# Filling TensorE's two gaps in the head: ten dummy matmuls in one group, two short ones ahead of the first transposes, six between the first and the second

## The chip, the cores and the metric

The kernel runs on one core of one Trainium2 chip. The metric is the device time of one execution in microseconds (us), as the median of several runs. A profiled execution is a separate run; it gives the page, the timeline and the waits.

## The reference

One block of a transformer over x of 2048 rows and 640 columns in bf16. The rows are layer-normalised; the sum of three terms is returned: x, a sliding-window attention with 32 heads of 20 columns and a window of 256, and a gated linear unit with 1536 hidden columns.

```python
x = A_x
xn = _layernorm(x, axis=-1)
return x + _A_ref(xn, A_wqkv, A_wo) + _B_ref(xn, B_w_gate, B_w_up, B_w_down)
# _A_ref: qkv = xn @ wqkv, masked softmax(q k^T / sqrt(20)) v per head, @ wo
# _B_ref: (sigmoid(xn @ w_gate) * (xn @ w_up)) @ w_down
```

## The kernel before

The 2048 rows are worked on in four chunks of 512 (`CW`), each of four blocks of 128 rows. A chunk needs its normalised rows transposed (`xnT`), with the columns of x on the partitions; then TensorE projects v (row block by row block), q and k (`proj_block`, tile `pqk`), takes scores (`scores`, tile `ps`), multiplies the exponentials with v (`pv`, tile `acc`), and computes the gated unit (`g_gu`, tiles `pg` and `pu`) and the output (tile `y`). The order on each engine is the order in which the program issues: a manual schedule. In the main part a list of filling work (`Fill`) is pulled between the steps of scores by costs that are fixed in the program, not by times on the chip.

The change lies in the head, which is the work on chunk 0 ahead of q and k and is written out by hand. SyncE's queue first loads the four row blocks of x (0, 1 and 3, then 2, each into a slice of `xc`), the weights of v in two halves, those of q and k, and the first halves of `wg` and `wu`. Meanwhile TensorE multiplies a constant tile of ones with itself, ten times with 512 columns (line 196, tile `pwarm`), with no use of the result. Row blocks 0 and 3 get mean and variance from VectorE (lines 205 and 211); row blocks 1 and 2 get theirs from ScalarE's accumulating activations (lines 637 and 642). The root comes from ScalarE (621, 643), the reciprocal and the normalisation from VectorE (631 and 224 for blocks 0 and 3, 647 and 648 for blocks 1 and 2). TensorE then transposes a block by five matmuls of 128 columns (line 230, tile `pt`), and ScalarE or VectorE copies the result into `xnT` (line 231). The projection of v (line 301, tiles `pv` and `pvh`) takes five matmuls of 320 columns for each block and half of the columns. The order on TensorE is: dummies, transposes of block 0, of block 1, five pv of block 0, five of block 1, transposes of block 3, five pv of block 0, five of block 3, five of block 1, transposes of block 2, five pv of block 3, ten of block 2, and then the fifty pqk of q and k.

In PSUM, `ps_d` has four buffers for everything with the tag "d", among them `pwarm`, `pv`, `pqk`, `pg`, `pu`, `acc` and `y`, which are taken in turn. In the head `ps_h` has four more for `pt` and `pvh`; later these banks belong to `ps`.

Behind the head SyncE loads chunk 1 of x (line 115), which needs the buffer of chunk 0 and so waits until block 2 has been normalised (line 648). GpSimd waits for that load (`landed`, line 700) and then clears parts of the scratch of q and k in HBM (line 153). The stores of q and k (line 271), the loads that spread them over partitions (`qT`, `kT`, line 284) and the second half of the first part of `w_up` (line 156) follow in SyncE's queue.

## Time and profile before

| | |
|---|---|
| runs | 309.94, 310.18, 310.60 us; median 310.18 |
| profiled execution | 310.91 us, of which 309.2 us from its first to its last instruction |
| busy TensorE | 305.0 us of 309.2 |
| busy VectorE, ScalarE, GpSimd | 186.3, 192.8 and 83.8 us |
| matmuls | 4431, as many weight loads |
| granted TensorE clock | 1.000 for the core |
| HBM | 25.59 MB read, 11.44 MB written |

Times in the views are in microseconds from the span's start. "PE" is TensorE's matmul side and "PEld" its weight loads, "DVE" VectorE, "ACT" ScalarE, "POOL" GpSimd, "SP" SyncE. Matmuls overlap one another in the array and their ends are modelled, so the length of a group holds, besides its work, the way of the last result through the array; the distance from one start to the next is the rate. An arrow names what ended a wait. A wait of TensorE is listed only where the engine was idle by these modelled ends.

### The profile page before, as it was taken

The numbers are of one execution on the slowest core, as the hardware profiler recorded it, in microseconds if no ns is written. First come the engines' busy times: TensorE is split into PE (matmuls) and PEld (weight loads), VectorE is DVE, ScalarE is ACT, GpSimd is POOL, SyncE is SP. The second block draws the span as 40 slices with busy tenths as digits, with TensorE's granted clock in tenths as the row PEclk, the third lists the DMA queues.
The fourth block names the chain that finished last, engine by engine and source line by source line (L and its number), as shares of the span: only waits on it lengthen the run. The fifth ranks groups of instructions, "written<-read, shape, count | busy, mean of one in ns | idle before, by whom it ended". The sixth has DMA issues, their size and how long they took to land.

```text
span 309.2 us, 10136 instructions
## 1 busy us (share of the span) xinstructions
PE 305.0 (99%) x4431; PEld 169.0 (55%) x4431; DVE 186.3 (60%) x373; ACT 192.8 (62%) x184; POOL 83.8 (27%) x183
## 2 busy tenths in 40 slices
PE   8999999999999999999999999999999999999996
PEld 3654445564556655644456655654446665444774
DVE  4577548678992679577564557355383626465523
ACT  6823686888764657777674656877676466768000
POOL 5011124554314133332223132331313232231100
PEclk9999999999999999999999999999999999999999
DMA  7996939879937322540252112560000210000301
GB/s 213 344 265 192 346 90 274 226 239 310 211 125 176 119 73 87 174 137 11 78 127 63 47 58 88 167 203 2 2 2 3 66 45 23 2 2 2 87 22 64
DMA packets 35756, 36.86 MB, mean 119 GB/s; under 512 B 2944, under 2 KB 35456, under 8 KB 35712
## 3 DMA queue, kind: packets, MB, share of 16 engines
q1 hardware_dynamic: 34304, 33.84, 37.1%
q0 software_dynamic: 544, 1.61, 1.7%
q10 hardware_dynamic: 864, 0.77, 0.9%
q8 instruction: 34, 0.56, 0.8%
q14 instruction: 10, 0.08, 0.1%
HBM read 25.59 MB, written 11.44 MB: 120 GB/s over the span
## 4 chain that ended last, share of the span: by engine, by line
PE 97%; DMA 1%; ACT 1%; DVE 0%; SPq 0%; issue 0%
PE pg L411 18%; PE y L434 17%; PE pu L420 17%; PE pqk L263 14%; PE ps L497 9%; PE y L441 7%; PE acc L530 6%; PE pv L321 6%; PE pv L301 2%; DMA xc<-in_A_x_dram 1%; PE pt L230 0%; PE pvh L301 0%; ACT turn L637 0%; ACT turn L642 0%; DVE turn L648 0%; SPq L132 0%
## 5 line engine op out<-in xcount | busy, mean ns | idle before, releaser
L503 ACT ACTIVATE pT<-ps 128x2048 bf16<-128x2048 f32 x76 | 141.1, 1856 | 61.8 <-PE ps L497 56.2
L486 POOL TENSOR_SCALAR_AFFINE_SELECT pT<-pT 64x256 bf16<-64x256 bf16 (+1 forms) x120 | 67.7, 564 | 183.4 <-ACT pT L503 132.7
L411 PE MATMUL pg<-xnT,wg 128*128 128x512 bf16 x240 | 59.9, 380 | 0.0
L420 PE MATMUL pu<-xnT,wu 128*128 128x512 bf16 x240 | 59.8, 380 | 0.0
L424 DVE SCALAR_TENSOR_TENSOR h<-th,pu 128x512 bf16<-128x512 f32 x48 | 32.8, 683 | 44.4 <-ACT th L414 25.9
L434 PE MATMUL y<-wd,h 128*128 128x320 bf16 (+2 forms) x396 | 57.0, 296 | 0.0
L263 PE MATMUL pqk<-xnT,wqkv 128*128 128x512 bf16 x200 | 45.9, 381 | 0.0
L434 PEld LDWEIGHTS <-h 128*128 128x128 bf16 x396 | 36.7, 98 | 16.3 <-issue 2.5
L514 DVE TENSOR_TENSOR pT<-pT,keep 128x512 bf16<-128x512 bf16 (+1 forms) x76 | 35.3, 465 | 13.9 <-ACT pT L503 13.0
L414 ACT ACTIVATE th<-pg 128x512 f32<-128x512 f32 x48 | 28.6, 595 | 14.8 <-PE pg L411 14.3
L420 PEld LDWEIGHTS <-wu 128*128 128x128 bf16 x240 | 22.3, 98 | 27.6 <-issue 2.0
L411 PEld LDWEIGHTS <-wg 128*128 128x128 bf16 x240 | 21.7, 98 | 27.0 <-issue 3.6
L263 PEld LDWEIGHTS <-wqkv 128*128 128x128 bf16 x200 | 22.5, 119 | 19.2 <-issue 1.8
L497 PE MATMUL ps<-qT,kT 20*64 20x320 bf16 (+4 forms) x1440 | 32.2, 261 | 0.0
L445 DVE SCALAR_TENSOR_TENSOR rows<-y,rows 128x320 bf16<-128x320 f32 x30 | 14.6, 489 | 24.9 <-PE y L441 24.8
L541 DVE STREAM_TRANSPOSE t<-acc 128x512 f32<-128x512 f32 x32 | 20.9, 692 | 12.1 <-PE acc L530 12.1
L497 PEld LDWEIGHTS <-kT 20*64 20x64 bf16 x1440 | 13.1, 103 | 23.0 <-issue 21.9
L441 PE MATMUL y<-wo,oc 128*128 128x320 bf16 (+2 forms) x165 | 24.2, 295 | 0.0
L530 PEld LDWEIGHTS <-v 64*32 64x32 bf16 x1440 | 17.0, 92 | 6.7 <-issue 1.8
L530 PE MATMUL acc<-pT,v 64*32 64x320 bf16 (+4 forms) x1440 | 20.0, 253 | 0.0
L441 PEld LDWEIGHTS <-oc 128*128 128x128 bf16 x165 | 15.5, 98 | 6.5 <-issue 1.0
L321 PE MATMUL pv<-wqkv,xnT 128*64 128x320 bf16 x240 | 17.4, 300 | 0.0
(61 smaller groups left out, 177.4 us busy)
## 6 DMA issues: line engine op xcount, KB each, us to landing
qT<-sq SPq DMA_DIRECT2D x16, 256.0 KB, 4.6
kT<-sk SPq DMA_DIRECT2D x16, 256.0 KB, 5.0
xc<-in_A_x_dram SPq DMA_DIRECT2D x16, 160.0 KB, 4.0
sq<-st SPq DMA_DIRECT2D x20, 128.0 KB, 3.5
sk<-st SPq DMA_DIRECT2D x20, 128.0 KB, 2.6
out_dram<-rows SPq DMA_DIRECT2D x15, 160.0 KB, 1.8
wg<-in_B_w_gate_dram SPq DMA_DIRECT2D x4, 480.0 KB, 7.3
wu<-in_B_w_up_dram SPq DMA_DIRECT2D x4, 480.0 KB, 8.2
```

The lines of the kernel that those rows point to most:

```text
L263: nc.tensor.matmul(ps, lhsT=wt[:, m, :], rhs=xnT[c][:, :, d, :], start=(d == 0), stop=(d == DC - 1))
L321: nc.tensor.matmul(ps[hf * U:(hf + 1) * U, 0:HALF], lhsT=xnT[c][:, s, d, rows], rhs=wqkv[:, d, 2 * D + hf * HALF:2 * D + (hf + 1) * HALF], ...
L411: nc.tensor.matmul(pg, lhsT=part(wg, d, f), rhs=xnT[c][:, :, d, :], start=(d == 0), stop=(d == DC - 1))
L420: nc.tensor.matmul(pu, lhsT=part(wu, d, f), rhs=xnT[c][:, :, d, :], start=(d == 0), stop=(d == DC - 1))
L424: nc.vector.scalar_tensor_tensor(out=h, in0=th, scalar=1.0, in1=pu, op0=ADD, op1=MULT)
L434: nc.tensor.matmul(y[:, 0:cut[1] - cut[0]], lhsT=ht[c, f][:, s * P:(s + 1) * P], rhs=wd[:, f, cut[0]:cut[1]], start=(f == 0), stop=False)
L441: nc.tensor.matmul(y[:, 0:cut[1] - cut[0]], lhsT=oc[c, m][:, s * P:(s + 1) * P], rhs=wo[:, m, cut[0]:cut[1]], start=False, stop=(m == DC - 1))
L486: nc.gpsimd.affine_select(out=part, in_=part, pattern=pattern, compare_op=GE, fill=0.0, base=-1 if sign > 0 else 0, channel_multiplier=sign)
L497: nc.tensor.matmul(ps[side * U:(side + 1) * U, i, col * U:(col + n) * U], lhsT=qk["k", kc, half][32 * i:32 * i + DH, 2 * r + side, kb * U: ...
L503: nc.scalar.activation(out=pt[:, :, 0:used, :], in_=ps[:, :, 0:used * U], func=EXP, scale=SCALE)
L514: nc.vector.tensor_tensor(out=part, in0=part, in1=limit.to_broadcast([P, HG, n * U]), op=MIN)
L530: nc.tensor.matmul(accs[side][32 * i:32 * i + 32, q * U:(q + n) * U], lhsT=vt[sb][rows, b, at:at + 32], rhs=pt[rows, i, col:col + n, :], s ...
```

## The change

The loop that issued the dummies in two groups of six and four becomes a function of the number and the columns. It is called with ten of 512 columns and two of 128 columns in the old place, that is ahead of the transposes of block 0, and with six of 128 columns between the transposes of block 0 and those of block 1. Each call takes a buffer with the tag "d" from `ps_d`, so three are taken instead of two. Nothing else is edited, and the number and the order of instructions on VectorE, ScalarE, GpSimd and SyncE are those of before; TensorE has eight matmuls and eight weight loads more. Behind the inserted lines the line numbers are higher by 4, and behind the call of six by 5.

```diff
-    for n in (6, 4):
+    def warm(n, cols):
         ps = ps_d.tile([P, CW], FP32, name="pwarm", tag="d")
         for k in range(n):
-            nc.tensor.matmul(ps, lhsT=ones[:, 0:P], rhs=ones, start=(k == 0), stop=(k == n - 1))
+            nc.tensor.matmul(ps[:, 0:cols], lhsT=ones[:, 0:P], rhs=ones[:, 0:cols],
+                             start=(k == 0), stop=(k == n - 1))
+
+    warm(10, CW)
+    warm(2, P)
...
     for lo, hi in ((0, 3), (3, DC)):
         transpose_rows(0, act, lo, hi)
+    warm(6, P)
     norm_act(1, xn1, neg1, r1)
```

## The prediction

> **What bounds the kernel now.** I read the page first, for the chain that ended last and the clock row, then TensorE's waits, then the timeline of TensorE over the first 14 us, and last the chain in order of time over the first 20 us. From the page, the second line of the chain (shares of the span by engine):

> ```profile
> PE 97%; DMA 1%; ACT 1%; DVE 0%; SPq 0%; issue 0%
> ```

> TensorE's waits over the whole span (who waited, for whom, us in total, times, longest):

> ```profile
> PE pwarm L196 <- PEq L826: 0.8, 1, 0.8
> PE pt L230 <- DVE turn L648: 0.4, 1, 0.4
> ```

> The end is set by TensorE's own instructions, and after 6.5 us it has no wait that the list shows. A microsecond taken off TensorE's start is then worth a microsecond at the end, as long as its operands come that much sooner too. The timeline of TensorE (start, length, engine, line, operation, output and inputs, count, and in brackets the idle time before):

> ```profile
> 0.85 4.42 PE L196 MATMUL pwarm<-const-bfloat16-1.0 128*128 128x512 bf16 x10 [0.85 <-PEq L826]
> 5.36 0.71 PE L230 MATMUL pt<-ident,turn 128*128 128x128 bf16 x5
> 6.50 0.71 PE L230 MATMUL pt<-ident,turn 128*128 128x128 bf16 x5 [0.43 <-DVE turn L648]
> 7.01 2.87 PE L301 MATMUL pv<-wqkv,xnT 128*128 128x320 bf16 x10
> ```

> Two gaps are to be seen: 0.09 us between the dummies' end (0.85 + 4.42 = 5.27) and the first transposes, and 0.43 us (6.07 to 6.50) before the second. The chain in order of time (start, length, what):

> ```profile
> 6.00 0.46 DVE turn L648
> 6.46 0.05 issue
> 6.50 0.71 PE pt L230 x5
> 7.22 2.67 PE pv L301 x10
> 9.88 0.46 PE pt L230 x5
> 10.35 1.44 PE pv L301 x10
> 11.79 0.68 PE pvh L301 x5
> 12.46 0.28 PE pt L230 x5
> 12.74 0.68 PE pvh L301 x5
> 13.42 1.44 PE pv L301 x10
> 14.86 5.18 PE pqk L263 x24
> ```

> Here is what the change can reach. The same matmul of 320 columns takes 2.67 / 10 = 0.267 us ahead of 9.88 and 0.68 / 5 = 0.136 us behind 11.79; five transposes fall from 0.71 to 0.28. The dummies of 512 columns go at 0.43 us (their weight loads start at 1.23, 1.66 and 2.08), the projections of the same width at 5.18 / 24 = 0.216. TensorE runs at half rate until about 10.1 us, inside the third set of transposes, although the page's granted clock reads 1.00 for the core; so this step is read from durations.

> **Why the step comes at 10.1.** The unbroken stretch of 4.42 us from 0.85 did not bring it, the one of 3.6 us from 6.50 did. Length alone cannot explain that; periods on a fixed grid can, if the rate rises at the end of a period that was (nearly) all work. One such period p ends at 10.1 and began no earlier than 6.50, so p is at most 3.6; that none fits between 0.85 and 5.27 rules out 2.42 to 3.08 (10.1 - 2p at most 5.27 and 10.1 - 3p at least 0.85). I take 3.08 to 3.6. The period before it then ends between 6.5 and 7.0 and began between 2.9 and 3.9: it held both gaps, some 0.5 us idle. This is worked out from one run, so it is an estimate.

> **The change part by part.** Ten dummies in one group instead of six and four: the same instructions, back to back already, worth nothing.

> Two of 128 columns, 0.43 x 128 / 512 = 0.107 us each, 0.21 together: the ten stop issuing at about 0.85 + 10 x 0.427 = 5.1, so the two issue until 5.3; the first transposes wait for VectorE's normalised row block 0 until 5.36. Hidden by that wait; without it they cost at most 0.21.

> Six of 128 columns, 0.64 us, queued behind the first transposes. Those stop issuing at about 5.9 (5.36 + 5 x 0.107), so the six end at 6.5, and the second transposes were waiting for L648 until 6.50. Cost 0 to 0.1 as the rows stand, at most 0.64 if row block 1 were ready at once. The second dummy group takes the bank of the old one, the third takes one more of the four "d" banks: every later tile moves one place round the ring and still follows the tile four before it. The order of instructions on VectorE, ScalarE, GpSimd and SyncE is unchanged, so nothing is queued behind a new wait.

> With both gaps filled TensorE works from 0.85 on, the period ending at 6.5 to 7.0 is full, and the rate doubles there instead of at 10.1. I follow the head with the step at 6.7. The second transposes' last result comes at 7.04 (7.22 before). VectorE's copy of it (0.49) starts behind L211 at 7.10 and ends at 7.59. The first five pv (0.136 each) are out by then, the next five run 7.65 to 8.33. Block 3 is normalised at 8.15 (7.85 + 0.45 = 8.30 before, 0.15 sooner with the copy); its transposes take 8.33 to 8.61, five pv 8.61 to 9.29. VectorE's copies (0.48 of v, 0.49 of the transposes, 0.48 of v) end at 8.65, 9.29 and 9.80, then it normalises block 2 by 10.42; ScalarE's root for it is there at 9.41 as before. Ten pv run 9.35 to 10.71, the last transposes to 10.99, copied by 11.68; the last fifteen pv run 10.99 to 13.10, with a wait of 0.07 for that copy. The first pqk started at 14.70 (14.86 in the chain is the end of the one before): it starts 1.6 us sooner. Half rate itself cost more, 10 x 0.131 for pv and some 0.6 for transposes, 1.9 in all; the rest goes to VectorE's and ScalarE's steps, which keep their lengths. My bounds for this term are 1.2 (step at 7.7, copies in the way) and 1.75.

> **What must come sooner too.** SyncE's loads of the head do not move. The q weights are issued at 3.71 and land 6.8 us later, at 10.5 (needed at 13.1); the k weights 8.5 later at 12.8 (needed at 18.5); block 1's x is waited for by GpSimd's L700 until 19.6, and behind it the two clears of scratch go out at 20.13 and 20.91. The k tile of the first scores is issued at 28.43, behind the last store of k, and lands 3.4 later at 31.8; the scores stand at 33.14. That is 1.3 us of cover, and the store, being released by TensorE's own results, moves with them. The narrowest is the second half of w_up: issued at 28.86, 4.4 to landing, 33.27, against its first use at 33.49. It follows the k tile in SyncE's queue and so moves too; if the stores move 0.3 less than TensorE, I lose up to 0.1 there. Taken as 0, bounds 0 and 0.3.

> Sum: -1.6 us. The profiled execution took 310.91 us (span 309.2); it would take 309.3. The three runs' median is 310.18, 0.73 lower; on that scale 308.6, with 308.4 to 309.3 from the bounds.

> **The rivals.**
> (a) The filling does not count. The full period 6.7 to 10.1 was 2.67 us of pv and the rest transposes; the filled one would be 2.6 us of dummies and 0.7 of transposes. If dummies on constant ones, or transposes, do not count as work, the step stays near 10.1 and the time at 310.2. Against it: the two periods are alike within 0.1 us in either count. [...]
> (b) The profiled execution is not like the others: the grid lies otherwise against the start, and the timed runs of the kernel before already have the early step. Then nothing is left to gain, 310.2. For it: all three are below the profiled one. Against it: the runs lie within 0.66 us, less than half of what the step is worth, and none is 1.6 below. [...]
> (c) The gain is taken back at the first scores: the stores of q and k, 1.6 us sooner, meet a DMA that the stage table shows full (share 1.08 to 1.12 until 20 us). If the k tile moved not at all, 33.14 - 1.6 = 31.54 against 31.8 would cost 0.3, and w_up at 33.27 against 31.9 would cost 1.4: 310.0 at the worst.
> (d) Slower: the step stays at 10.1 and the dummies stand in front of transposes that are ready. It decides where x lands sooner than in this profile, so that block 1 is normalised before 6.4. Price up to 0.64 for the six and 0.21 for the two: 310.9 where most of it counts. Against it: L648 ended at 6.46 here, behind a chain through ScalarE.

> **How the numbers follow.** About 0.2% (0.62 us) is what a measurement of this kernel can tell from no change, so faster means below 309.56, slower above 310.80. Forecast 0.74; (a) 0.09, (b) 0.06 and (c) 0.04, which all end within 0.2%; (d) 0.07. The first is faster, 0.74; the next three 0.19; the last slower, 0.07. The range goes from 307.9 (the upper bound 1.75, and the runs' own spread) to 310.3, so that it takes in the rivals that gain nothing and leaves out (d).

> **What would show it.** In the changed kernel's timeline: dummies and transposes without a gap before 6.5; the ten pv behind the second transposes in some 1.5 us instead of 2.87; the first pqk near 13.1; the first scores near 31.5; no wait of TensorE at L420 or L497 ahead of 35 us. It is wrong if pv still takes 0.267 us up to 10 us (a or d), if the early step is there and the time unchanged (b), or if a wait for kT or wu appears (c).

## The result, and the profile after

The changed kernel is slower, by about 0.35%: 310.55 us median (309.73 to 312.72, 21 runs) against 309.28 us (309.19 to 310.9, 21 runs, the three of before among them), ratio 1.0035 with a 95% interval of 1.0022 to 1.0048. The kernel before, in its further runs, is mostly faster than its first three: 12 of the 21 lie between 309.19 and 309.31. The changed kernel never reaches that, and spreads over 3 us.

Its profiled execution is one of its quick ones, 309.82 us with a span of 308.0. The chain by engine, from its page:

```profile
PE 97%; DMA 1%; ACT 1%; DVE 0%; issue 0%; SPq 0%
```

The timeline of TensorE (start, length, what, count, idle before):

```profile
0.85 4.22 PE L196 MATMUL pwarm<-const-bfloat16-1.0 128*128 128x512 bf16 x12 [0.85 <-PEq L831]
5.29 0.45 PE L234 MATMUL pt<-ident,turn 128*128 128x128 bf16 x5 [0.22 <-DVE turn L228]
5.58 0.51 PE L196 MATMUL pwarm<-const-bfloat16-1.0 128*128 128x128 bf16 x6
6.43 0.45 PE L234 MATMUL pt<-ident,turn 128*128 128x128 bf16 x5 [0.34 <-DVE turn L652]
6.72 1.60 PE L305 MATMUL pv<-wqkv,xnT 128*128 128x320 bf16 x10
```

Twelve dummies now take 4.22 us where ten took 4.42, and the first transposes are already at full rate (0.45 for five, against 0.71 before): the step came during the ten wide dummies, at some 4.5 (their starts lie 0.43 us apart up to 4.22, then 0.36, and the next start follows 0.22 later), ahead of everything that was added. The six then fill only half of their gap. The chain in order of time says what the head gained:

```profile
6.43 0.45 PE pt L234 x5
6.88 1.44 PE pv L305 x10
...
13.11 10.79 PE pqk L267 x50
```

By this view, which counts from the end of the matmul before, the pqk start 1.75 us sooner (13.11 against 14.86). But the last matmul comes only 1.24 us sooner. TensorE's waits show where 0.5 us went, in the line with "issue", which the kernel before did not have:

```profile
PE pwarm L196 <- PEq L831: 0.8, 1, 0.8
PE pu L424 <- issue: 0.3, 1, 0.3
PE pt L234 <- DVE turn L652: 0.3, 1, 0.3
PE pt L234 <- DVE turn L228: 0.2, 1, 0.2
```

and in the chain for 128 to 136 us (start, length, what):

```profile
133.01 0.36 PE ps L501 x24
133.37 0.32 PE pu L424
133.69 0.35 issue
134.04 1.04 PE pu L424 x4
```

Between the first and the second of five matmuls of one accumulation TensorE stands still, with no semaphore to wait for ("issue"). From start to start it is 0.74 us instead of 0.22, so 0.52 is lost. One thing that such a wait does not name is the supply of the instructions themselves. Section 3 of the page has a DMA queue for them (queue and kind: packets, MB, share):

```profile
q8 instruction: 34, 0.56, 0.8%
```

In the trace each has 16384 bytes, and they follow TensorE's progress: from packet 0, when 217 instructions had been executed, to packet 33, at 8646, one starts for every 255.4 on average, matmuls, weight loads and a few of its sequencer together (packet 13 at 3535, packet 14 at 3790; packets are counted from 0). That a packet holds 256 instructions is my estimate from this. The stall comes after 3776 of the instructions in the trace.

### The profile page after: what moved, and what is told of

Same layout as the page of the kernel before. It is cut to its first block, busy times and chain, and to the rows that moved or that the text cites. A ratio compares the mean times of both kernels' runs of the same rounds, so it can differ in the third digit from the quotient of the medians.

```text
span 308.0 us, 10152 instructions
## 1 busy us (share of the span) xinstructions
PE 303.3 (98%) x4439; PEld 168.3 (55%) x4439; DVE 186.1 (60%) x373; ACT 192.4 (62%) x184; POOL 83.8 (27%) x183
## 4 chain that ended last, share of the span: by engine, by line
PE 97%; DMA 1%; ACT 1%; DVE 0%; issue 0%; SPq 0%
PE pg L415 18%; PE y L438 18%; PE pu L424 17%; PE pqk L267 15%; PE ps L501 9%; PE y L445 7%; PE acc L534 6%; PE pv L325 6%; PE pv L305 1%; DMA xc<-in_A_x_dram 1%; PE pvh L305 0%; PE pt L234 0%; ACT turn L641 0%; ACT turn L646 0%; DVE turn L652 0%
## 5 line engine op out<-in xcount | busy, mean ns | idle before, releaser
L501 PEld LDWEIGHTS <-kT 20*64 20x64 bf16 x1440 | 13.1, 103 | 23.2 <-issue 21.6
```

Source lines behind the costliest of these rows:

```text
L501: nc.tensor.matmul(ps[side * U:(side + 1) * U, i, col * U:(col + n) * U], lhsT=qk["k", kc, half][32 * i:32 * i + DH, 2 * r + side, kb * U: ...
```

## The experiments

**Theory F**: the 16 added instructions (eight matmuls, eight weight loads) move the borders of TensorE's code packets against a burst of short matmuls, so that a packet comes late. **Rivals**: E, the earlier head collides with DMA later; G, the short dummies themselves; and (b) of the prediction on what the head is worth. Each ratio below is against runs of the kernel before made beside the experiment; their medians lie between 309.44 and 309.64, where beside the changed kernel it was 309.28, so medians of different sets are comparable to some 0.3 us only.

**Sixteen instructions elsewhere.** The kernel before, its head untouched, with the first scores issued twice:

```diff
-            for side in range(2):
+            again = 1 if (c, pr, k, q) == (0, 0, 0, 0) else 0
+            for side in [0, 1] * (1 + again):
```

> The kernel before, with the eight matmuls of the first scores issued twice (0.12 us by 24 in 0.36); its head is that of before, but behind 31 us TensorE's instruction stream stands 16 instructions further on, as in the changed kernel. Theory F (code fetch: TensorE's stream is loaded in packets of 16 KB, and 16 more instructions move the packets' borders into a burst of short matmuls, where the next packet comes late): as spread as the changed kernel, median some 310.2 to 310.8, against 309.2 to 309.4 of before; in the profile a stall of TensorE of 0.3 to 1 us without a releaser near 135 us. Rival E (the earlier head itself collides with DMA later): like before plus 0.12, 309.3 to 309.5, no stall.

310.76 us (309.99 to 312.73, 12 runs), ratio 1.0028 (1.0009 to 1.0047). Its wait list has the stall at the same instruction, 3776, although no dummy was added and the head is that of before, which neither E nor G allows:

```profile
PE pu L420 <- issue: 0.7, 1, 0.7
```

**The changed head without the shift.** The changed kernel less eight matmuls with v:

```diff
         for n_, (pt, k, q, n, col) in enumerate(flat):
+            if (c, pr, n_) == (0, 0, 4):
+                continue
```

> The changed kernel without eight of the matmuls with v of chunk 0's first pair of heads (0.11 us by 92 in 1.26; that key block's part of the sum is left out): the head is the changed one, but behind 48 us the instruction stream is aligned as before. Theory F: tight again, 309.0 to 309.3, without the long tail, and below before's median by the share of before's runs that had the late step. Rival E: as the changed kernel less 0.1, 310.3 to 310.6.

309.42 us (309.04 to 310.05, 12 runs), ratio 0.9987 (0.9972 to 1.0002), 0.1 above the range expected. The head is all there, the spread of 3 us has become 1, and the whole list of TensorE's waits is one line:

```profile
PE pwarm L196 <- PEq L833: 0.8, 1, 0.8
```

With 0.11 us for the work left out this is some 1.0 us below the changed kernel's median, and 1.4 us by the two ratios: this is what the alignment costs.

**The number of dummies.** The same filling with six instructions more than before, and 18 dummies without filling:

```diff
-    warm(2, P)
+    warm(1, 2 * P)
...
-    warm(6, P)
+    warm(1, CW)
+    warm(1, 2 * P)
```

> The changed kernel with the same filling in fewer matmuls: one of 256 columns instead of the two, one of 512 and one of 256 instead of the six; 6 instructions more than before instead of 16. Theory F: another alignment, so another time: between 309.2 and 310.5, without a better forecast. Rival E: as the changed kernel, 310.5. Rival G (short dummies themselves disturb the rate or the transposes): 309.2.

310.07 us (309.44 to 310.81, 12 runs), ratio 1.0005 (0.9991 to 1.002).

```diff
-    for n in (6, 4):
+    for n in (9, 9):
...
-            nc.tensor.matmul(ps, lhsT=ones[:, 0:P], rhs=ones, start=(k == 0), stop=(k == n - 1))
+            nc.tensor.matmul(ps[:, 0:284], lhsT=ones[:, 0:P], rhs=ones[:, 0:284],
+                             start=(k == 0), stop=(k == n - 1))
```

> The kernel before with its dummies cut into eighteen of 284 columns instead of ten of 512 (the same columns to 8), so 16 instructions more from the start and both gaps left open. Theory F: as the changed kernel or slower, 310.3 to 310.9, with a stall near 135 us. Rival E and rival G: as before, 309.2 to 309.4.

310.50 us (309.81 to 311.68, 12 runs), ratio 1.0028 (1.0012 to 1.0045). With both gaps open it is as slow as the changed kernel, so the filling is not what costs. Both profiles have the stall at 3776, and a second wait, for the operand that the prediction had named as the one with the narrowest cover; here with 18 dummies:

```profile
PE pu L421 <- issue: 0.4, 1, 0.4
PE pu L421 <- DMA wu<-in_B_w_up_dram: 0.4, 1, 0.4
```

**A larger shift.** The ten wide dummies cut into thirty, and the open gaps with thirty-eight; both 56 instructions more than before:

```diff
-    warm(10, CW)
+    warm(30, 170)
```

> The changed kernel with the ten dummies of 512 columns cut into thirty of 170 (the same columns to 20), so 56 instructions more than before instead of 16. Theory F: the borders of packets 13, 22 and 26 lie well away from the bursts, no stall, 309.0 to 309.3, with none of before's runs at 310 and more: the gaps' filling alone is seen. Rival (any added instruction costs, by its number): slower than the changed kernel, 311 or more.

309.47 us (309.14 to 309.82, 12 runs), ratio 0.9983 (0.9967 to 0.9998): more instructions than the changed kernel, and a little faster than both kernels, though 0.2 above the range expected.

```diff
-    for n in (6, 4):
+    for n in (19, 19):
...
-            nc.tensor.matmul(ps, lhsT=ones[:, 0:P], rhs=ones, start=(k == 0), stop=(k == n - 1))
+            nc.tensor.matmul(ps[:, 0:135], lhsT=ones[:, 0:P], rhs=ones[:, 0:135],
+                             start=(k == 0), stop=(k == n - 1))
```

> The kernel before with its ten dummies cut into thirty-eight of 135 columns, both gaps left open: 56 instructions more, as with thirty. Theory F and rival (b) of the prediction together: no stall, but now and then the late step of the rate, so a lowest time of 309.1 as with the gaps filled, and a tail to 310.5 in about a third of the runs; the distance of the two medians is what filling the gaps is worth, 0.1 to 0.4. If my forecast's 1.6 held for most runs, this one would lie 1.2 or more above it.

309.57 us (309.2 to 311.3, 12 runs), ratio 0.9989 (0.997 to 1.0007). Neither profile has the stall. At this alignment the medians with and without filling differ by 0.1 us, less than the intervals; one run of the twelve with open gaps was above 310, where a third had been expected in the tail. The profile with open gaps shows what else limits an early step, as the first pv waited for the weights of v:

```profile
PE pv L302 <- DMA wqkv<-in_A_wqkv_dram: 0.4, 1, 0.4
```

**The kernel before again.** Three further profiles.

> The kernel before, for a second profile. Rival (b): the step of the rate comes elsewhere than at 10.1, most likely ahead of 7 us, the span is 307.5, and TensorE's stream has no stall near 135 us. My forecast needed the step at 10.1 again.

310.89 us, span 309.2, the step at 10.1 as in the profile of the prediction, against what was expected.

> The kernel before, for another profile. Rival (b): the step of the rate comes ahead of 7 us in most runs; then 309.2 to 309.6 and a span near 307.6. If the step stands at 10.1 as in the two profiles so far: 310.9.

309.35 us, span 307.6, with the step during the first transposes:

```profile
5.38 0.52 PE L230 MATMUL pt<-ident,turn 128*128 128x128 bf16 x5
6.51 0.45 PE L230 MATMUL pt<-ident,turn 128*128 128x128 bf16 x5 [0.61 <-DVE turn L648]
6.80 1.60 PE L301 MATMUL pv<-wqkv,xnT 128*128 128x320 bf16 x10
```

> As before_look2: 309.2 to 309.6 with the step ahead of 7 us, 310.9 with the step at 10.1.

309.76 us, span 308.1, the step between the two sets of transposes (0.71, then 0.45), and the stall in the kernel before itself, also behind instruction 3776, which is eight matmuls further on in the program, as it has 16 instructions less ahead:

```profile
134.40 1.03 PE L411 MATMUL pg<-xnT,wg 128*128 128x512 bf16 x4
135.85 0.39 PE L411 MATMUL pg<-xnT,wg 128*128 128x512 bf16 x1 [0.43 <-issue]
```

So 310.9 is this kernel with the late step and 309.3 with an early one. Two of its four profiles have the late step, but by the times the profile that I predicted from was of the rarer kind: of the 98 runs of the kernel before beside the experiments 13 have a span of 309.0 or more. Its alignment is not safe either, only better.

**Why the packet is late.** Two theories are tried. F1: a burst of short matmuls uses 256 instructions up faster than any packet comes. F2: the packet stands in the DMA engines behind the 2 MB of q and k that are loaded for chunk 2 just then. The first attempt moved the call for the later half of these loads in the program:

```diff
-            if s == 1 and c > 1:
+            if s == (3 if c == 2 else 1) and c > 1:
```

> The changed kernel, its instructions all kept, but the last four loads of q and k for chunk 2 (1 MB) are issued two row blocks of v later. Theory F2 (the packet of instructions that TensorE runs dry for, near 133 us, is late because it stands behind 2 MB of q and k in the DMA engines): the packet comes before the burst, no stall near 133 us, 309.1 to 309.5. Rival F1 (it is late only because 256 instructions with a burst in them are used up faster than any packet comes): stall and spread as in the changed kernel, 310.3 to 310.7.

310.45 us (309.37 to 311.11), ratio 1.0012 (0.9994 to 1.003). The edit did nothing: the order on every engine, SyncE's too, is that of the changed kernel, as nothing else stands in SyncE's queue there to hold the loads back. It tells nothing of F1 or F2. It counts as a second measurement of the changed kernel, 0.98 us above that of the thirty dummies, which was taken beside it. Its profile (311.11 us) has two stalls, which cost 1.1 and 0.8 us from start to start:

```profile
PE pu L424 <- issue: 1.0, 1, 1.0
PE pwarm L196 <- PEq L831: 0.8, 1, 0.8
PE acc L534 <- issue: 0.7, 1, 0.7
```

The second attempt puts four of the eight loads (1 of 2 MB) behind ScalarE's work, where they leave from 134.6 us on:

```diff
-            if s == 1 and c > 1:
+            if s == 1 and c > 2:
...
-            nc.sync.dma_start(out=to[:, r % 2], in_=src[:, r])
+            queue.dma_start(out=to[:, r % 2], in_=src[:, r])
...
-mix(g_gu(1, 3, 12), norms3, 0, 2)
+mix(itertools.chain(g_gu(1, 3, 5), later(spread_rest, 2, nc.scalar), g_gu(1, 5, 12)), norms3, 0, 2)
```

> The changed kernel, TensorE's instructions all kept; the last four loads of q and k for chunk 2 (1 MB of 2) go through ScalarE's queue, two steps of the gated unit later, so that they leave behind the burst of short matmuls near 132 us. ScalarE issues them, some 0.5 us each, off TensorE's path. Theory F2 (the packet of instructions comes late because it stands behind 2 MB of q and k): packet 13 starts within 1 us of its border instead of 1.7 to 2.4, no stall near 133 us, 309.1 to 309.6. Rival F1 (256 instructions with a burst in them are used up faster than any packet comes): the stall and the spread stay, 310.3 to 310.7.

309.66 us (309.28 to 311.57, 12 runs), ratio 1.001 (0.9991 to 1.003), just above the range expected of F2. Four of 12 runs lie above 310, against 18 of 21 of the changed kernel at 310.0 or above; more on these four below. The stretch of 130 to 132 us (busy time of each engine, the clock, the DMA share, GB/s) of the changed kernel, and then of this one:

```profile
130.00:132.00 2.00, 2.00 (x33) 0.90 (x38) 1.11 (x2) 1.75 (x2) 0.79 (x4) 1.00 1.00 342
```

```profile
130.00:132.00 2.00, 2.00 (x25) 0.96 (x25) 0.81 (x2) 1.88 (x2) 1.28 (x4) 1.00 0.05 13
```

The DMA is full in the one and empty in the other, and the stall near 133 us is gone. The table follows packet 13 in the traces: when TensorE reached instruction 3521 (the border 256 ahead of the stall), when the packet started, when TensorE reached 3777, and what the stall there cost:

| kernel | at 3521 | packet starts | at 3777 | lost |
|---|---|---|---|---|
| changed | 129.86 | 131.59 | 134.03 | 0.52 |
| first scores twice | 130.26 | 132.34 | 134.76 | 0.85 |
| 18 dummies | 130.31 | 132.15 | 134.53 | 0.57 |
| 13 dummies, filled | 131.40 | 133.14 | 135.38 | 0.53 |
| changed, loads moved in vain | 130.69 | 133.09 | 135.48 | 1.14 |
| before, `before_look3` | 131.69 | 133.47 | 135.85 | 0.59 |
| before, profile of the prediction | 133.43 | 134.60 | 137.00 | 0 |
| before, `before_look2` | 131.77 | 131.91 | 135.12 | 0 |
| 30 dummies, filled | 129.22 | 130.34 | 133.64 | 0 |
| loads through ScalarE | 130.82 | 130.46 | 134.26 | 0 |

Wherever TensorE ran dry there it went on 2.24 to 2.44 us after the packet's start. In the eight profiles without this stall 2.40 to 4.41 us lay between the packet's start and instruction 3777; the least of them, 2.40, is the profile of the prediction, which was just in time. The burst (91 acc and 24 ps, 230 of the 256 instructions, in 1.62 us) leaves a late packet too little time. What varies is the start: 1.7 to 2.4 us behind the border in the six profiles that stalled, from 0.4 ahead of it to 1.6 behind in the eight others, and it is early with the loads moved. The kernel before shows the same with no edit at all: in the profile of `before_look3` the DMA engines ran out of loads by 132.1 but for one, which moved one packet of 1024 bytes after another until 133.47, and the code packet starts there. That is theory F2 for this packet; the burst of F1 makes it matter. One stall stayed in the profile with the loads through ScalarE, at 81.7 us, behind instruction 1984, with another packet (3776 - 1984 is 7 x 256):

```profile
PE acc L534 <- issue: 0.8, 1, 0.8
```

**Both remedies at once.** Thirty dummies, and the loads through ScalarE.

> Both remedies at once: the ten wide dummies cut into thirty (56 instructions more than before), and the last four loads of q and k for chunk 2 through ScalarE's queue, behind the burst. Theory F with F2: no stall near 133 us for either reason, 309.1 to 309.5 in every run, at or below the thirty dummies alone (309.14 to 309.82). If what is left of the spread there came from something else than packets, no better than it.

309.65 us (309.5 to 310.96, 12 runs), ratio 1.0015 (1.0001 to 1.0028): not what was expected. Its profile (309.51 us, span 307.7) has no stall at all, yet four runs were above 310.3. They lost their time between the first and the last instruction (spans of 308.5 to 309.1, the others 307.7 to 308.1), but by what stays open; another packet and a late step are both possible. So thirty dummies alone are the best version found, and its lead of 0.17% is at the edge of what can be told.

The head of this profile is close to the one that the prediction drew, with both gaps filled and the step behind them, at 6.9:

```profile
5.29 0.72 PE L234 MATMUL pt<-ident,turn 128*128 128x128 bf16 x5
5.80 0.85 PE L196 MATMUL pwarm<-const-bfloat16-1.0 128*128 128x128 bf16 x6
6.44 0.65 PE L234 MATMUL pt<-ident,turn 128*128 128x128 bf16 x5
6.92 1.60 PE L305 MATMUL pv<-wqkv,xnT 128*128 128x320 bf16 x10
```

Up to 6.9 TensorE had done nothing but dummies and transposes, so these can bring the step. With the gaps open, the profile of the prediction had no step there and waited until 10.1. Over all profiles the step came at 6.9 or sooner in the seven with filled gaps, and in five of the seven with open ones. That fits the prediction's mechanism, but is too few to show it.

**A second place: the end of the program.** Each run's time is longer than its span from the first to the last instruction. For the 98 runs of the kernel before beside the experiments the difference is 1.66 to 1.78 us, and it is at most 1.84 with 6 or 56 instructions more (all loads on SyncE's queue) and with the shift undone. With exactly 16 more it spreads: up to 2.72 in the changed kernel (above 1.8 in 11 of 21 runs), 2.79 with the first scores twice, 2.67 with 18 dummies, and 3.01 and 3.47 in the two slowest runs with the loads through ScalarE, whose spans of 308.3 and 308.1 are short. The traces with 16 more hold 8897 instructions of TensorE, and 8897 is 3777 + 20 x 256: if a packet holds 256, the stream ends at a border. In the profiles of the first scores twice and of 18 dummies one more code packet starts behind the span, at 310.92 and 310.29 us with spans of 308.7 and 308.4. So a part of the changed kernel's loss, up to some 1 us in single runs, lies behind its last instruction, and code is the likely cause; no run moved the end alone. Its median is mostly lost ahead of that: the median span is 308.7, and 307.7 to 307.9 for the kernel before. The two kernels with loads through ScalarE have at least 1.79 in every run, which stays unexplained.

## Why the prediction was wrong, point by point

- **The end is TensorE's.** Right: 1.75 us off the head moved TensorE's work behind it by 1.7 up to 133 us; no operand came late in the changed kernel's profile. The narrowest cover was rightly named (w_up, 0.3 to 0.4 us of waiting in two experiments, where I took 0 with a bound of 0.3).
- **The head's term.** In the profile 1.75 us for a forecast of 1.6 with bounds of 1.2 to 1.75. But there it was luck, and not the filling: the step came ahead of it.
- **The grid.** The step that failed first: from one execution I placed the periods against the kernel's start and took that place for all runs. The runs show steps at some 4.5, during the first transposes, between the two sets, at 6.9 and at 10.1. So the edges that I had put at 10.1 and at 6.5 to 7.0 belong to single executions. The periods were my estimate from one trace, and no run shows them. In `before_look3` the step came between the two sets with the first gap open (some 0.2 us from the last dummy to the first transposes), so if there are periods, one with that gap in it can do, where I had asked for a (nearly) full one. Rival (b), to which I gave 0.06, is what happened to the gain: by their times most runs of before had the early step already.
- **Its price in the median.** I carried 1.6 us from the profiled execution to the median, 0.73 below it. That difference was the sign that the profile had the late step. At equal alignment (56 instructions more) the filling moved the median by 0.1, less than the intervals.
- **The cost of the added matmuls.** The step that made the kernel slower, a term of the sum that was mis-sized: I gave the eight pairs 0 to 0.1 us, by the time that they take on TensorE, and priced neither their place in the instruction stream nor the code queue that the page lists. It measured 1.0 to 1.4 us in the median (changed kernel against the one with the shift undone), which is the whole of the loss of 1.27.
- **Rival (a)** (the filling does not count) could not be seen in the changed kernel's profile, where the step came before it. The step at 6.9 behind dummies and transposes alone, in the profile with both remedies, speaks against it; whether the transposes alone would count stays open. **Rival (c)** put a collision at the q and k loads of the first scores; it was the loads of chunk 2, and what they held up was code. **Rival (d)** had the kernel slower, as it was, but by another mechanism: in its profile the second transposes still waited 0.3 us for VectorE behind the dummies.

## What to carry to other kernels

This kernel of some 8,900 TensorE instructions has a hidden operand, its code. In one like it, count the instructions that an edit adds, look for "issue" waits of TensorE between matmuls of one group, and test an edit's idea at a second alignment before believing its time, for better or worse. Take the rate at the start from several profiles, not from one, and where the profiled execution lies above the median by more than the runs agree, ask first what it had that they had not.
